# One order of work and one size of transfer: the attention stage of a fused attention, soft-MoE and SwiGLU kernel

## The chip, the core and the metric

The kernel runs on one core of a Trainium2 chip. The metric is the device time of one execution in microseconds (us). One execution of each kernel is also recorded by the hardware profiler; the rows shown below come from that record. The engines are PE (matrix products and transposes), DVE, ACT and POOL (element work), and SP, which here only issues transfers.

## What is computed

Three layers follow each other. The inputs q, k, v are float32, 8 batches x 8 heads x 576 positions x 64.

```python
# 1. attention inside chunks of 64 positions
scores = q_c @ k_c.T / sqrt(64)
attn = exp(scores - rowmax); attn /= attn.sum(-1) + 1e-9
out = attn @ v_c
x = out as 4608 tokens x 512
# 2. soft mixture of 8 experts with 4 slots each, hidden 1024
logits = x @ phi                       # 4608 x 32
d = softmax of logits over the tokens; slot_input = d.T @ x
slot_out[e] = relu(slot_input[e] @ w1[e]) @ w2[e]
c = softmax of logits over the slots;  x = c @ slot_out
# 3. SwiGLU with weights of 512 x 1536
out = (silu(x @ w_gate) * (x @ w_val)) @ w_out
```

## The kernel before, in words

The 4608 tokens are 36 tiles of 128 tokens. The attention stage works on pairs of tiles, 18 pairs in all (`NP = NTILE // 2`). Text below numbers the pairs 0 to 17.

The instructions of every engine stand in the order in which the Python code emits them; no scheduler moves them. Each engine takes its own in that order and waits where a value or a buffer is not there yet. All transfers are issued by SP, in order too: a transfer that waits holds up those behind it.

The steps of a pair, with the names of their tiles and their lines:

- `emit_scores` (L321): 64 small products on PE into `s_ps` (L328), then on DVE a maximum `m` (L336) and a subtraction to `ssb` (L338). Behind a tile's products stands the load of the q and k tile that takes its buffer (`load_qk`, L284).
- `emit_pt` (L347), once for each tile: four transposes of `ssb` into `pt_ps` (L351), and the exponential on ACT (L353).
- `emit_pv` (L358): the products with v into `xa_ps` and `xb_ps` (L365), with the load of the next v tile that takes the buffer (`load_v`, L287), and the normalisation on DVE to `x_sb` (L381 to L388).
- `emit_xt` (L395), once for each tile: four transposes of `x_sb` into `xt_ps` (L401), copied by ACT (L403).
- For a group of four tiles: `emit_logits` (products of `xt` with phi into `lt_ps`, L420, a maximum on DVE, exponentials on ACT, the last of them the copy `lt_all`, L453), then `emit_et` (one transpose into `e_ps`, L466) and `emit_si` (products of the exponentials with `x_sb` into `si_ps`, L484, added up by DVE).
- `spread_v` (L316): v must stand in a block-diagonal form; POOL copies the lower 64 rows to their place (L318) and clears where they were (L319).

The PSUM tiles `pt_ps`, `xt_ps`, `lt_ps`, `e_ps` and `si_ps` take turns in a pool of three buffers (`ps_t`).

The loop at L545 emits, in turn `k` (with `a = k - 1`): the v products of pair `a`; logits or slot sums of an earlier group; the score transposes of pair `k`; the scores of pair `k + 1` and the spread of its v; the x transposes of pair `a - 1`; `emit_et`. q, k and v have buffers for four tiles each. The text calls the stretch from one pair's v products to the next a turn. In three of four turns `pump(1)` (L141) also issues the load of an expert weight (1 MB): sixteen buffers of the pool `wp` are filled while attention runs. When the loop is over, the q, k, v buffers become four more weight buffers (`wx`, L572).

After the loop a tail (L576 to L599) finishes the last x transposes, the last two groups and the maximum over all tokens. The expert stage (L758) takes the weights in the order `order`, L130, and each weight buffer that it frees takes a further load. The SwiGLU stage follows (L921 on); the change does not touch it.

Of the kernel before, what the change touches and what calls it, by code (L numbers as in the profile page):

```python
# [8 lines left out]
F32 = mybir.dt.float32  # L9
# [24 lines left out]
def tile_attn_softmoe_swiglu(  # L34
# [10 lines left out]
    out: bass.AP,  # L45
):
    nc = tc.nc
    D = v.shape[4] - 1
    NT, DM = out.shape
    E = w1.shape[0]  # L50
    NS = phi.shape[1]
    NTILE = NT // 128
# [4 lines left out]
    VW = D + 1  # L57
# [210 lines left out]
    with tc.manual_schedule():  # L268
# [8 lines left out]
        pa = ExitStack()  # L277
        ring = pr.enter_context(tc.tile_pool(name="ring", bufs=1, side="right"))

        NK, NV = 4, 4  # L280
        qk_sb = [ring.tile([128, 2, 4, 128], F32, name=f"qk{i}") for i in range(NK)]
        v_bd = [ring.tile([128, 2, 2, 4, VW], F32, name=f"vbd{i}") for i in range(NV)]

        def load_qk(u):  # L284
            nc.sync.dma_start(out=qk_sb[u % NK], in_=qk[u])

        def load_v(u):  # L287
            nc.sync.dma_start(out=v_bd[u % NV][:, 0], in_=v[u])

        for i in (0, 1):  # L290
            load_qk(i)
        for i in (0, 1):
            load_v(i)
        for i in (2, 3):
            load_qk(i)
        nc.sync.dma_start(out=phi_sb, in_=phi.rearrange("(k p) s -> p k s", p=128))
        for i in (2, 3):
            load_v(i)

        make_identity(nc, ident)  # L300
        for i in range(NV):
# [11 lines left out]
        sc_t = {}  # L313
        row = [slice(0, 64), slice(64, 128)]

        def spread_v(u):  # L316
            t = v_bd[u % NV]
            nc.gpsimd.tensor_copy(out=t[row[1], 1], in_=t[row[1], 0])  # L318
            nc.gpsimd.memset(t[row[1], 0], 0.0)  # L319

        def emit_scores(p):  # L321
            sp = ps_s.tile([128, 2, 2, 4, 64], F32, tag="s", name="s_ps")
            for n in range(8):
                i, j = 2 * p + n // 4, n % 4
                for a in range(2):
                    for cc in range(2):
                        t = slice(64 * cc, 64 * cc + 64)
                        nc.tensor.matmul(  # L328
                            out=sp[t, a, n // 4, j, :], lhsT=qk_sb[i % NK][row[a], 0, j, t],
                            rhs=qk_sb[i % NK][row[a], 1, j, t], start=True, stop=True,  # L330
                        )
                if j == 3 and i + NK < NTILE:
                    load_qk(i + NK)
            sv = sp.rearrange("p a t j k -> p a (t j) k")
            m = sm.tile([128, 2, 8], F32, tag="m", name="m", bufs=1)
            nc.vector.tensor_reduce(out=m, in_=sv, axis=AX.X, op=ALU.max)  # L336
            ssb = atp.tile([128, 8, 2, 64], F32, tag="ssb", name="ssb", bufs=1)
            nc.vector.tensor_tensor(  # L338
                out=ssb.rearrange("p n a k -> p a n k"), in0=sv,
                in1=m.unsqueeze(3).to_broadcast([128, 2, 8, 64]), op=ALU.subtract,  # L340
            )
            for t in range(2):
                sc_t[2 * p + t] = ssb[:, 4 * t:4 * t + 4]
# [14 lines left out]
        def emit_pv(p):  # L358
            xa = ps_x.tile([128, 2, 512], F32, tag="xa", name="xa_ps")
            xb = ps_x.tile([128, 512], F32, tag="xb", name="xb_ps")  # L360
            banks = [xa[:, 0], xa[:, 1], xb]
            for n in range(8):
                i, j = 2 * p + n // 4, n % 4
                for cc in range(2):
                    nc.tensor.matmul(  # L365
                        out=banks[n // 3][64 * cc:64 * cc + 64, (n % 3) * 2 * VW:(n % 3 + 1) * 2 * VW],
                        lhsT=pt_t[i][:, j, 64 * cc:64 * cc + 64],
                        rhs=v_bd[i % NV][:, :, cc, j, :],
                        start=True, stop=True,
                    )  # L370
                if j == 3:
                    pt_t.pop(i)
                    if i + NV < NTILE:
                        load_v(i + NV)
            x = xp.tile([128, 2, 512], F32, tag="x", name="x_sb")
            rec = sm.tile([128, 16, 1], F32, tag="rec", name="rec", bufs=2)
            av = xa[:, :, 0:6 * VW].rearrange("p b (h d) -> p b h d", d=VW)
            bv = xb[:, 0:4 * VW].rearrange("p (h d) -> p h d", d=VW)
            ra, rb = rec[:, 0:12].rearrange("p (b h) o -> p b h o", b=2), rec[:, 12:16]
            xv = x.rearrange("p t (h d) -> p (t h) d", d=D)  # L380
            nc.vector.tensor_scalar(out=ra, in0=av[:, :, :, D:VW], scalar1=1e-9, scalar2=None, op0=ALU.add)  # L381
            nc.vector.tensor_scalar(out=rb, in0=bv[:, :, D:VW], scalar1=1e-9, scalar2=None, op0=ALU.add)
# [28 lines left out]
        lt_t = {}  # L411
        lx_t = {}

        def emit_lmm(g, lt=None):
            if lt is None:
                lt = ps_t.tile([128, 512], F32, tag="t", name="lt_ps")
            lt_t[g] = lt
            for kk in range(4):
                for jt in range(4):
                    nc.tensor.matmul(  # L420
# [35 lines left out]
        def emit_logits(g):  # L456
            emit_lmm(g)
            emit_lmax(g)
            emit_lexp(g)
# [77 lines left out]

        warm(6)
        spread_v(0)
        spread_v(1)  # L540
        emit_scores(0)
        load_gv0(0, wp)
        warm(4)
        NP = NTILE // 2
        for k in range(NP + 1):  # L545
            a = k - 1
            if a >= 0:
# [1 line left out]
            if k == NP:  # L549
                break  # L550
            if a >= 3 and a % 2:
                emit_logits((a - 3) // 2)
            elif a >= 4:
                emit_si((a - 4) // 2)
            emit_pt(2 * k)
            emit_pt(2 * k + 1)
            if k + 1 < NP:
                emit_scores(k + 1)
                spread_v(2 * k + 2)
                spread_v(2 * k + 3)  # L560
            if a >= 1:
                emit_xt(2 * a - 2)
                emit_xt(2 * a - 1)
            if a >= 3 and a % 2:
                emit_et((a - 3) // 2)
            if k == 0 or k % 4 != 3:
                pump(1)
            elif k + 1 == NP - 2:
# [450 lines left out]
```

## Time and profile before

| What | Value |
|---|---|
| Time, median of 3 runs | 545.08 us (544.49 to 547.83) |
| The profiled execution's own time | 543.5 us |
| Its span, first to last instruction | 541.7 us |
| PE busy | 521.3 us, 96% of the span |
| DVE busy | 406.7 us, 75% |
| ACT, POOL busy | 260.4 us and 252.9 us |
| Granted PE clock, mean | 0.996 |
| Read from HBM | 80.95 MB |
| Transfers of q and k | 36 of 512 KB, landing 6.6 us after the issue (median) |
| Transfers of v | 36 of 260 KB, landing after 7.5 us |
| Transfers of the expert weights | w1: 16 of 1 MB, 9.3 us; w2: 15 of 1 MB, 13.5 us |

How to read it: a share of busy time is a mean over stages with different limits. Up to about 119 us the kernel is in the attention loop, to 130 us in the tail, to 170 us in the expert stage, and from there in SwiGLU. A wait is put down to whatever came last. PE can be shown as busy in a stage whose length something else sets, since a product that waits for its weights inside a group of products is merged into it.

### The profile page before, as it was taken

To read this page: it belongs to the slowest core of one execution; us is meant where nothing else is said; L and a number is where in the kernel's file an instruction comes from. 1 tells how busy PE (TensorE), PEld (TensorE's weight loads), DVE (VectorE), ACT (ScalarE), POOL (GpSimd) and SP (SyncE) were. 2 spreads that over 40 slices of the span, in tenths; PEclk is the share of its full clock that TensorE was granted. 3 is DMA by queue.
4 is the path that set the end of the run, shared out by engine and by line. 5 is a ranking of instruction groups with operands and counts; after the bars stand their busy time and mean duration, and the time that the engine had idled before them with its cause. 6 is when DMAs were issued, how large, how long until landed. Compare 5 with 4: busy or idle time off the path is not lost.

```text
span 541.7 us, 11039 instructions
## 1 busy us (share of the span) xinstructions
PE 521.3 (96%) x4389; PEld 409.8 (76%) x4389; DVE 406.7 (75%) x673; ACT 260.4 (48%) x504; POOL 252.9 (47%) x252
## 2 busy tenths in 40 slices
PE   7899999998998889999999999999999999999997
PEld 6778887873335568888888888888888888888885
DVE  5778987864766999888898889989898943433554
ACT  1344533342447766666565555545654533333331
POOL 3333343321002576576566756656664743343342
PEclk9999999999999989999999999999999999999999
DMA  8999999999999502020202220222000000222344
GB/s 324 404 358 398 348 405 347 413 416 400 421 416 417 247 1 77 2 78 2 77 1 77 77 79 0 79 79 77 0 1 0 3 0 1 77 79 77 113 179 174
DMA packets 23762, 91.09 MB, mean 168 GB/s; under 512 B 3104, under 2 KB 3104, under 8 KB 17696
## 3 DMA queue, kind: packets, MB, share of 16 engines
q1 hardware_dynamic: 23712, 90.40, 43.1%
q8 instruction: 34, 0.56, 0.4%
q14 instruction: 16, 0.13, 0.1%
HBM read 80.95 MB, written 9.44 MB: 167 GB/s over the span
## 4 chain that ended last, share of the span: by engine, by line
PE 81%; DVE 9%; DMA 6%; issue 2%; ACT 1%; POOL 0%; SPq 0%; ACTq 0%; DVEq 0%
PE o L891 18%; PE o L893 18%; PE o L892 18%; DMA w2t<-in_moe_w_dram 6%; PE v_ps L847 4%; PE g_ps L847 4%; PE xa_ps L365 4%; PE xt_ps L401 3%; PE s_ps L328 3%; PE pt_ps L351 2%; PE gg_ps L828 2%; PE si_ps L484 1%; DVE ssb L338 1%; DVE m L336 1%; PE h_ps L652 1%
## 5 line engine op out<-in xcount | busy, mean ns | idle before, releaser
L860 POOL TENSOR_TENSOR lo_sb<-s_sb,hi_sb 128x512 fp32r<-128x512 f32 x106 | 140.5, 1326 | 130.9 <-ACT hi_sb L859 127.9
L891 PE MATMUL o<-whl,hi_sb 128*128 128x512 f32 x428 | 167.7, 392 | 2.5 <-DVE part L900 2.5
L893 PE MATMUL o<-whl,lo_sb 128*128 128x512 f32 x428 | 167.2, 391 | 0.5 <-POOL lo_sb L860 0.5
L892 PE MATMUL o<-whl,hi_sb 128*128 128x512 f32 x428 | 167.1, 390 | 0.0
L850 ACT ACTIVATE s_sb<-g_ps 128x512 f32<-128x512 f32 (+1 forms) x110 | 64.7, 590 | 149.9 <-PE g_ps L847 147.7
L851 DVE TENSOR_TENSOR s_sb<-s_sb,v_ps 128x512 f32<-128x512 f32 (+1 forms) x110 | 74.0, 674 | 74.5 <-ACT s_sb L850 73.2
L891 PEld LDWEIGHTS o<-whl,hi_sb 128*128 128x128 f32 x428 | 80.6, 188 | 22.2 <-DVE part L900 4.5
L893 PEld LDWEIGHTS o<-whl,lo_sb 128*128 128x128 f32 x428 | 80.6, 188 | 17.8 <-POOL lo_sb L860 0.9
L892 PEld LDWEIGHTS o<-whl,hi_sb 128*128 128x128 f32 x428 | 80.6, 188 | 16.3
L859 ACT ACTIVATE hi_sb<-s_sb 128x512 fp32r<-128x512 f32 (+1 forms) x110 | 67.6, 616 | 0.8 <-DVE s_sb L851 0.8
L904 DVE TENSOR_TENSOR part<-part,o 128x512 f32<-128x512 f32 x92 | 57.1, 677 | 2.6 <-PE o L893 2.6
L318 POOL COPY vbd<-vbd 64x520 f32<-64x520 f32 x36 | 22.3, 619 | 69.9 <-DMA vbd<-in_v_dram 56.2
L213 POOL TENSOR_TENSOR mt<-mt,ex 128x512 f32<-128x512 f32 x32 | 39.5, 1234 | 27.5 <-PE g_ps L847 13.8
L200 DVE SCALAR_TENSOR_TENSOR ex<-raw,ex 128x512 uint16<-128x512 uint16 x32 | 47.2, 1477 | 0.1
L847 PE MATMUL v_ps<-c_t,g_st 128*128 128x512 f32 (+1 forms) x110 | 42.5, 390 | 0.8 <-DMA raw<-in_moe_w_val_dram 0.5
L847 PE MATMUL g_ps<-c_t,g_st 128*128 128x512 f32 (+1 forms) x110 | 42.4, 389 | 0.1
L353 ACT ACTIVATE pt<-pt_ps 128x512 f32<-128x512 f32 x36 | 19.5, 596 | 36.2 <-PE pt_ps L351 36.2
L195 DVE SCALAR_TENSOR_TENSOR mt<-mt,raw 128x512 f32<-128x512 f32 x32 | 34.9, 1090 | 0.0
L336 DVE TENSOR_REDUCE m<-s_ps 128x16 f32<-128x1024 f32 x18 | 22.0, 1224 | 14.8 <-PE s_ps L328 14.7
L187 DVE TENSOR_SCALAR mt<-raw 128x512 int32<-128x512 int32 x32 | 32.9, 1027 | 0.0
L365 PE MATMUL xa_ps<-vbd,pt 128*64 128x130 f32 x432 | 28.2, 277 | 0.0
L403 ACT ACTIVATE xt<-xt_ps 128x512 f32<-128x512 f32 (+1 forms) x36 | 19.3, 596 | 13.7 <-PE xt_ps L401 10.2
(138 smaller groups left out, 664.2 us busy)
## 6 DMA issues: line engine op xcount, KB each, us to landing
qk<-in_qk_dram SPq DMA_DIRECT2D x36, 512.0 KB, 6.6
w1t<-in_moe_w_dram SPq DMA_DIRECT2D x16, 1024.0 KB, 9.3
w2t<-in_moe_w_dram SPq DMA_DIRECT2D x15, 1024.0 KB, 13.5
vbd<-in_v_dram SPq DMA_DIRECT2D x36, 260.0 KB, 7.5
out_dram<-part SPq DMA_DIRECT2D x36, 256.0 KB, 2.2
raw<-in_moe_w_out_dram SPq DMA_DIRECT2D x6, 1024.0 KB, 7.1
raw<-in_moe_w_gate_dram SPq DMA_DIRECT2D x5, 1024.0 KB, 4.8
raw<-in_moe_w_val_dram SPq DMA_DIRECT2D x5, 1024.0 KB, 5.1
```

What stands on the lines that cost most here:

```text
L200: nc.vector.scalar_tensor_tensor(out=ex, in0=hh, scalar=0x8000, in1=ex, op0=ALU.bitwise_and, op1=ALU.bitwise_or)
L213: nc.gpsimd.tensor_tensor(out=m, in0=m, in1=p, op=ALU.mult)
L365: nc.tensor.matmul(out=banks[n // 3][64 * cc:64 * cc + 64, (n % 3) * 2 * VW:(n % 3 + 1) * 2 * VW], lhsT=pt_t[i][:, j, 64 * cc:64 * cc + 64 ...
L847: nc.tensor.matmul(out=ps[:, k], lhsT=g_st[:, c, gi, ff:ff + 128], rhs=c_blk(b)[:, k], start=True, stop=True)
L850: nc.scalar.activation(out=s[:, k], in_=gp[:, k], func=ACTF.Silu)
L851: nc.vector.tensor_tensor(out=s[:, k], in0=s[:, k], in1=vp[:, k], op=ALU.mult)
L859: nc.scalar.activation(out=hi[:, k], in_=s[:, k], func=ACTF.Copy)
L860: eng.tensor_tensor(out=lo[:, k], in0=s[:, k], in1=hi[:, k].bitcast(F32), op=ALU.subtract)
L891: nc.tensor.matmul(out=a, lhsT=hi[:, ts], rhs=w_hi, start=first, stop=False)
L892: nc.tensor.matmul(out=a, lhsT=hi[:, ts], rhs=w_lo, start=False, stop=False)
L893: nc.tensor.matmul(out=a, lhsT=lo[:, ts], rhs=w_hi, start=False, stop=last)
L904: nc.vector.tensor_tensor(out=p[:, t], in0=p[:, t], in1=a, op=ALU.add)
```

## The change

Two things are done in the attention stage.

First, transfers. The arrays of q and k, and of v, are laid out by pairs on the host side, and one transfer brings a pair: 1 MB for q and k, 520 KB for v. There are two buffers of a pair each in place of four of a tile, so the memory is the same. Only the very first pair of q and k still comes in two transfers. A pair's load is issued when the whole pair in its buffer has been used. The spread of v is one copy and one clearing for a pair.

Second, the order in a turn. The x transposes move from the turn's end to the place right behind the v products, with `emit_et` ahead of them. The logits and the slot sums move behind the score transposes, and each is done one turn sooner. So the next-to-last group's logits are done inside the loop, and the tail loses one round of logits with its own PSUM buffer (`lt2`).

```diff
-        NK, NV = 4, 4
-        qk_sb = [ring.tile([128, 2, 4, 128], F32, name=f"qk{i}") for i in range(NK)]
-        v_bd = [ring.tile([128, 2, 2, 4, VW], F32, name=f"vbd{i}") for i in range(NV)]
-        def load_qk(u):
-            nc.sync.dma_start(out=qk_sb[u % NK], in_=qk[u])
-        def load_v(u):
-            nc.sync.dma_start(out=v_bd[u % NV][:, 0], in_=v[u])
+        NK, NV = 2, 2
+        qk_sb = [ring.tile([128, 2, 2, 4, 128], F32, name=f"qk{i}") for i in range(NK)]
+        v_bd = [ring.tile([128, 2, 2, 2, 4, VW], F32, name=f"vbd{i}") for i in range(NV)]
+        def load_qk(p):
+            for t in (slice(0, 1), slice(1, 2)) if p == 0 else (slice(0, 2),):
+                nc.sync.dma_start(out=qk_sb[p % NK][:, t], in_=qk[p][:, t])
+        def load_v(p):
+            nc.sync.dma_start(out=v_bd[p % NV][:, 0], in_=v[p])
...
         def emit_scores(p):
...
-                if j == 3 and i + NK < NTILE:
-                    load_qk(i + NK)
+            if p + NK < NP:
+                load_qk(p + NK)
...
         def emit_pv(p):
...
                 if j == 3:
                     pt_t.pop(i)
-                    if i + NV < NTILE:
-                        load_v(i + NV)
+            if p + NV < NP:
+                load_v(p + NV)
...
             if a >= 3 and a % 2:
-                emit_logits((a - 3) // 2)
-            elif a >= 4:
-                emit_si((a - 4) // 2)
-            emit_pt(2 * k)
-            emit_pt(2 * k + 1)
-            if k + 1 < NP:
-                emit_scores(k + 1)
-                spread_v(2 * k + 2)
-                spread_v(2 * k + 3)
+                emit_et((a - 3) // 2)
             if a >= 1:
                 emit_xt(2 * a - 2)
                 emit_xt(2 * a - 1)
-            if a >= 3 and a % 2:
-                emit_et((a - 3) // 2)
+            emit_pt(2 * k)
+            emit_pt(2 * k + 1)
+            if a >= 2 and a % 2 == 0:
+                emit_logits((a - 2) // 2)
+            elif a >= 3:
+                emit_si((a - 3) // 2)
+            if k + 1 < NP:
+                emit_scores(k + 1)
+                spread_v(k + 1)
...
         g = NG - 1
-        lt2 = ps_s.tile([128, 2, 512], F32, tag="s", name="lt_ps")
+        emit_et(g - 1)
         emit_xt(NTILE - 4)
         emit_xt(NTILE - 3)
-        emit_lmm(g - 1, lt2[:, 0])
+        emit_si(g - 1)
         emit_xt(NTILE - 2)
-        emit_lmax(g - 1)
         emit_xt(NTILE - 1)
-        emit_lexp(g - 1)
-        emit_lmm(g, lt2[:, 1])
-        emit_et(g - 1, False)
+        emit_lmm(g)
         emit_lmax(g)
         emit_lexp(g)
-        emit_zst(g - 1)
         emit_m1()
-        emit_si(g - 1)
         emit_et(g, False)
```

The order on PE in the middle of the loop, before: two turns, from the v products of an odd pair (`xa_ps`) on. `vbd` and `qk` are the buffers of v and of q and k, one for a tile.

```order
L420 MATMUL lt_ps<-xt,phi_sb 32x128 x16
L351 MATMUL pt_ps<-ident,ssb 128x128 x8
L328 MATMUL s_ps<-qk_99 64x64 x16
L328 MATMUL s_ps<-qk_100 64x64 x16
L401 MATMUL xt_ps<-ident,x_sb 128x128 x8
L466 MATMUL e_ps<-ident,et 128x128
L365 MATMUL xa_ps<-vbd_101,pt 64x130 x8
L365 MATMUL xa_ps<-vbd_102,pt 64x130 x4
L365 MATMUL xb_ps<-vbd_102,pt 64x130 x4
L484 MATMUL si_ps<-x_sb,e 32x512 x4
```

And the same place now:

```order
L363 MATMUL xa_ps<-vbd_99,pt 64x130 x12
L363 MATMUL xb_ps<-vbd_99,pt 64x130 x4
L399 MATMUL xt_ps<-ident,x_sb 128x128 x8
L349 MATMUL pt_ps<-ident,ssb 128x128 x8
L416 MATMUL lt_ps<-xt,phi_sb 32x128 x16
L326 MATMUL s_ps<-qk_97 64x64 x32
L363 MATMUL xa_ps<-vbd_100,pt 64x130 x12
L363 MATMUL xb_ps<-vbd_100,pt 64x130 x4
L462 MATMUL e_ps<-ident,et 128x128
L399 MATMUL xt_ps<-ident,x_sb 128x128 x8
L349 MATMUL pt_ps<-ident,ssb 128x128 x8
L480 MATMUL si_ps<-x_sb,e 32x512 x4
```

The scores, which had the x transposes behind them, are now the last work of a turn, and the logits stand between the score transposes and the scores.

On POOL, the spread of one pair of v before, and then now; the number behind `vbd` is the buffer:

```order
L318 COPY vbd2_103<-vbd2_103 64x520
L319 MEMSET vbd2_103 64x520
L318 COPY vbd3_104<-vbd3_104 64x520
L319 MEMSET vbd3_104 64x520
```

```order
L316 COPY vbd1_100<-vbd1_100 64x1040
L317 MEMSET vbd1_100 64x1040
```

Two short steps for each tile became one of twice the length for the pair, behind one transfer.

## Rows read from the trace of the kernel before

**Rows 1.** Chain of waits, 128 to 180 us; start, length, what.

```profile
153.21 15.51 DMA w2t<-in_moe_w_dram
168.76 0.69 PE so_ps L695 x13
```

**Rows 2.** Stretches: engines' busy us, granted clock, transfer share, GB/s (last).

```profile
12.00:18.00 6.00, 5.23 (x126) 4.59 (x120) 5.17 (x9) 1.09 (x2) 1.57 (x3) 1.00 1.03 408
84.00:86.00 2.00, 2.00 (x73) 1.93 (x73) 0.80 (x2) 1.94 (x7) 1.88 (x4) 1.00 0.67 227
88.00:90.00 2.00, 2.00 (x21) 1.01 (x16) 1.17 (x3) 0.10 (x1) 1.88 (x4) 1.00 1.03 338
96.00:102.00 6.00, 5.90 (x119) 4.33 (x118) 4.08 (x11) 2.92 (x9) 1.71 (x4) 1.00 1.02 410
132.00:138.00 6.00, 6.00 (x56) 1.85 (x52) 3.98 (x19) 1.14 (x3) 0.33 (x3) 1.00 0.99 386
162.00:168.00 6.00, 6.00 (x56) 1.78 (x48) 3.53 (x6) 4.48 (x7) 1.48 (x1) 1.00 1.02 416
```

**Rows 3.** Timeline of SP's issues, 80 to 86 us; start, time to issue, what.

```profile
80.77 1.27 SPq L288 DMA_DIRECT2D vbd<-in_v_dram  x2
84.76 1.10 SPq L285 DMA_DIRECT2D qk<-in_qk_dram  x2
85.92 0.42 SPq L89 DMA_DIRECT2D w1t<-in_moe_w_dram  x1
```

**Rows 4.** Timeline of PE, two turns: start, us, what, idle before.

```profile
66.94 1.55 PE L365 MATMUL xa_ps<-vbd,pt 128*64 128x130 f32 x24
...
68.86 1.08 PE L420 MATMUL lt_ps<-xt,phi_sb 128*32 128x128 f32 x32
69.87 1.09 PE L351 MATMUL pt_ps<-ident,ssb 128*128 128x128 f32 x8
70.89 1.16 PE L328 MATMUL s_ps<-qk 64*64 64x64 f32 x64
72.29 1.14 PE L401 MATMUL xt_ps<-ident,x_sb 128*128 128x128 f32 x8 [0.24 <-ACT lt_all L453]
73.27 0.32 PE L466 MATMUL e_ps<-ident,et 128*128 128x128 f32 x1
73.52 1.55 PE L365 MATMUL xa_ps<-vbd,pt 128*64 128x130 f32 x24
...
79.58 1.55 PE L365 MATMUL xa_ps<-vbd,pt 128*64 128x130 f32 x24
```

**Rows 5.** Timeline of PE, an earlier odd turn, first row to next turn.

```profile
28.89 1.55 PE L365 MATMUL xa_ps<-vbd,pt 128*64 128x130 f32 x24
...
35.50 1.55 PE L365 MATMUL xa_ps<-vbd,pt 128*64 128x130 f32 x24
```

**Rows 6.** Timeline of DVE, beside the first turn of rows 4.

```profile
72.12 1.23 DVE L336 TENSOR_REDUCE m<-s_ps 128x16 f32<-128x1024 f32 x1 [0.59 <-PE s_ps L328]
73.38 1.23 DVE L338 TENSOR_TENSOR ssb<-s_ps,m 128x1024 f32<-128x1024 f32 x1
```

**Rows 7.** Timeline of PE, up to the v products of pair 2.

```profile
18.74 1.09 PE L351 MATMUL pt_ps<-ident,ssb 128*128 128x128 f32 x8 [0.68 <-DVE ssb L338]
...
21.37 0.50 PE L328 MATMUL s_ps<-qk 64*64 64x64 f32 x18 [0.69 <-issue]
...
22.83 1.55 PE L365 MATMUL xa_ps<-vbd,pt 128*64 128x130 f32 x24
```

**Rows 8.** Timeline of POOL: the spread of pair 2, first and last.

```profile
21.30 0.61 POOL L318 COPY vbd<-vbd 64x520 f32<-64x520 f32 x1 [7.67 <-DMA vbd<-in_v_dram]
...
23.12 0.53 POOL L319 MEMSET vbd<- 64x520 f32 x1
```

**Rows 9.** The tile vbd, 20 to 120 us: its transfers, one for a tile.

```profile
DMA to landing us min/median/max: 5.1/7.5/9.2
```

**Rows 10.** Timeline of PE in the tail: the last group's logits.

```profile
123.62 1.08 PE L420 MATMUL lt_ps<-xt,phi_sb 128*32 128x128 f32 x32 [1.02 <-ACT lt_all L453]
```

More of the change, by code (lines that the diff above doesn't have):

```diff
@@ L47, in tile_attn_softmoe_swiglu @@
     nc = tc.nc
-    D = v.shape[4] - 1
+    D = v.shape[5] - 1
     NT, DM = out.shape
@@ L278, in tile_attn_softmoe_swiglu @@
         ring = pr.enter_context(tc.tile_pool(name="ring", bufs=1, side="right"))
-        NK, NV = 4, 4
-        qk_sb = [ring.tile([128, 2, 4, 128], F32, name=f"qk{i}") for i in range(NK)]
-        v_bd = [ring.tile([128, 2, 2, 4, VW], F32, name=f"vbd{i}") for i in range(NV)]
-        def load_qk(u):
-            nc.sync.dma_start(out=qk_sb[u % NK], in_=qk[u])
-        def load_v(u):
-            nc.sync.dma_start(out=v_bd[u % NV][:, 0], in_=v[u])
[L290 to L295, printed above, removed]
+        NK, NV = 2, 2
+        NP = NTILE // 2
+        qk_sb = [ring.tile([128, 2, 2, 4, 128], F32, name=f"qk{i}") for i in range(NK)]
[5 more added lines that the diff above has]
+            nc.sync.dma_start(out=v_bd[p % NV][:, 0], in_=v[p])
+        load_qk(0)
+        load_v(0)
+        load_qk(1)
         nc.sync.dma_start(out=phi_sb, in_=phi.rearrange("(k p) s -> p k s", p=128))
-        for i in (2, 3):
-            load_v(i)
+        load_v(1)
         make_identity(nc, ident)
@@ L314, in tile_attn_softmoe_swiglu, with spread_v @@
         row = [slice(0, 64), slice(64, 128)]
-        def spread_v(u):
-            t = v_bd[u % NV]
+        def spread_v(p):
+            t = v_bd[p % NV]
             nc.gpsimd.tensor_copy(out=t[row[1], 1], in_=t[row[1], 0])
@@ L323, in emit_scores @@
             for n in range(8):
-                i, j = 2 * p + n // 4, n % 4
+                j = n % 4
                 for a in range(2):
@@ L328, in emit_scores @@
                         nc.tensor.matmul(
-                            out=sp[t, a, n // 4, j, :], lhsT=qk_sb[i % NK][row[a], 0, j, t],
-                            rhs=qk_sb[i % NK][row[a], 1, j, t], start=True, stop=True,
-                        )
-                if j == 3 and i + NK < NTILE:
-                    load_qk(i + NK)
+                            out=sp[t, a, n // 4, j, :], lhsT=qk_sb[p % NK][row[a], n // 4, 0, j, t],
+                            rhs=qk_sb[p % NK][row[a], n // 4, 1, j, t], start=True, stop=True,
+                        )
+            if p + NK < NP:
+                load_qk(p + NK)
             sv = sp.rearrange("p a t j k -> p a (t j) k")
@@ L367, in emit_pv @@
                         lhsT=pt_t[i][:, j, 64 * cc:64 * cc + 64],
-                        rhs=v_bd[i % NV][:, :, cc, j, :],
+                        rhs=v_bd[p % NV][:, :, n // 4, cc, j, :],
                         start=True, stop=True,
@@ L412, in tile_attn_softmoe_swiglu, with emit_lmm @@
         lx_t = {}
[L414 to L417, printed above, removed]
+        def emit_lmm(g):
+            lt = lt_t[g] = ps_t.tile([128, 512], F32, tag="t", name="lt_ps")
             for kk in range(4):
@@ L539, in tile_attn_softmoe_swiglu @@
         spread_v(0)
-        spread_v(1)
         emit_scores(0)
@@ L543, in tile_attn_softmoe_swiglu @@
         warm(4)
-        NP = NTILE // 2
         for k in range(NP + 1):
@@ L993 @@
             a = _np.stack([qt.reshape(NU, 128, 4, 128), kt.reshape(NU, 128, 4, 128)], 2)
+            a = a.reshape(NU // 2, 2, 128, 2, 4, 128).transpose(0, 2, 1, 3, 4, 5)
         elif name == "v":
@@ L996 @@
             a = _np.concatenate([a, _np.ones(a.shape[:-1] + (1,), a.dtype)], -1).transpose(0, 2, 1, 3, 4)
+            a = a.reshape(NU // 2, 2, 128, 2, 4, D + 1).transpose(0, 2, 1, 3, 4, 5)
         elif name in ("moe_w1", "moe_w2"):
```

## The prediction

> **What bounds the kernel now.** I read the chain of waits first, from the expert stage backwards. The SwiGLU stage can start only when the last expert weight is there: two links of over 15 us on transfers of w2 stand before 168.76 us [rows 1]. What follows is bound by PE, and the change does not touch it. So the change is worth what it does to the moment when that last weight lands.
>
> Then the stretches, to see when the transfers are the limit [rows 2]. From 96 us on they run at 410 GB/s or more with a share of 1.02, and only 132 to 138 us shows 386. A queue that is full all the time cannot end sooner unless it was filled sooner or moves faster. Ahead of 96 us it was not always full: in one of four turns no weight is loaded, and behind such a turn there is a hole. The last hole is at 84 to 86 us, 227 GB/s and a share of 0.67. It ends when SP asks for the next q and k at 84.76 us and a weight at 85.92 us [rows 3]. So the end of the expert stage hangs on the time of these two issues, and they hang on how far PE has come in the loop.
>
> Then the timeline of PE. A turn has v products (1.92 us, from 66.94 to 68.86), logits or slot sums (1.01), score transposes (1.02), scores (about 1.1) and x transposes (0.98), in sum 6.0, and in every second turn 0.25 for `e_ps` [rows 4]. An even turn takes 6.06 us: PE has no slack there. An odd turn takes 6.58, so 0.27 of it is waiting; the first such turn takes 6.61 [rows 5], 0.30 of it waiting. The row of the x transposes names the cause: 0.24 us for the copy `lt_all`, which has to give back a PSUM buffer.
>
> The profiled execution took 543.5 us, 1.6 below the median of 545.08. Sums are made against it, and 1.6 is added at the end.
>
> **The change, step by step**, up to the last hole.
>
> *The wait of the odd turns.* Between `lt_ps` and the third use of that buffer now stand scores and v products, some 3 us, in place of score transposes and scores, and ACT is through with its copy by then. I take the wait as gone: four odd turns before the hole, 4 x 0.29 = -1.15 us.
>
> *What the moved x transposes do to the score transposes.* These need `ssb`, which is there 3.72 us after the scores began (70.89 [rows 4] to 74.61 [rows 6]). In the new order scores, v products and x transposes take 1.1 + 1.92 + 0.98 = 4.0 us ahead of them. The cover was one logits longer; 0.3 us is left. Nothing, then, unless DVE comes late to the scores.
>
> *The logits, one turn sooner.* One more round stands before any place in the loop: +1.01 us [rows 4]. The tail gives it back, but the tail is behind the hole.
>
> *v by pairs, first time.* Pair 2 is the first whose v is reloaded. Its first tile had landed by 21.30 us, both were spread at 23.12 + 0.53 = 23.65, and the v products of the first tile began at 22.83, before the second was ready [rows 7, 8]. Now nothing can begin before both are spread. The queue is full there (408 GB/s [rows 2]), so the second tile's 0.27 MB land 0.65 us behind the first, at 21.95; the spread of both takes 2.35 (23.65 - 21.30); start at 24.3, 1.5 us later than before. PE would be there earlier, since the x transposes fill the 0.68 us in which it waited for `ssb` [rows 7]. At the other end, if the larger transfer lands sooner, the cost is 0. I take +1.1, nearer to the row.
>
> *v by pairs, later.* A pair's load is issued when its buffer's v products are done, and is needed two turns later: 2 x 6.18 - 1.92 = 10.4 us, and less 2.35 for the spread 8.1 are left to land. A tile took 7.5 us in the median and 9.2 at most [rows 9]. The load of a pair is issued 0.95 later than that of its first tile and lands 0.65 behind it, so 7.2 in the median and 8.9 at most: in most turns nothing, in the worst 0.8. I take +0.3 before the hole, between 0 and 1.0. [...]
>
> *The issues move in the turn.* Scores, and the load of q, k and the weight behind them, now come after the x transposes: about 1.0 us later in the turn. v does not move.
>
> At the hole v is thus asked for 1.1 + 1.0 - 1.15 + 0.3 = 1.3 us later, q, k and the weight 2.3 later. The hole is as long as q, k and the weight make it, less what the later v puts into it; I take the middle, **+1.8 us**, between -0.1 and +3.4.
>
> *Behind the hole.* After it the rate is low even at a full share: 338 GB/s at 88 to 90 us with 1.03 [rows 2]. Two us at 416 in its place would be 0.4 us; if all of 86 to 94 us were like this row and larger transfers cured it, 1.5. I take -0.4. The low stretch at 132 to 138 us costs (416 - 386) / 416 x 6 = 0.4 us [rows 2]; it comes when the tail keeps PE from freeing weight buffers. The tail loses one logits (1.01 us) and a wait of 1.02 [rows 10] and so comes no later than before: -0.4. Six MB of q, k and v are still to come behind the hole; at 416 in place of 410 GB/s that is -0.2. The SP issues saved (36 of about 0.4 us) cost nothing now, since SP waits, and POOL's work stays the same in sum.
>
> Sum: 1.8 - 0.4 - 0.4 - 0.2 = +0.8 us, so 544.3 for an execution like the profiled one, **545.9 us** for the median. The tail's saving does not reach the end otherwise: the weights are not there yet.
>
> **The rivals.**
>
> *Larger transfers make the queue faster (542.9 us).* For it: 408 to 410 GB/s with q, k and v in the mix against 416 with weights alone, and the 338 above [rows 2]. Then pair 2 costs nothing, v is never late, the issues come 0.9 us later, and behind the hole 1.5 + 0.4 + 0.2 come back: -1.2; and if the first hole's delay in the turn is hidden by work still in the queue, -2.2, which with 1.6 is 542.9. Against it: 408 is only 2% short. [...]
>
> *v is late in nearly every turn (551.2 us, slower).* Place: the start of the v products, behind POOL. If the landing is over 8.1 us behind the end of the v products, PE waits for the whole excess every second turn. At 9.2 us, the longest of a tile, plus 0.2 for the issue, two turns must last 1.92 + 0.2 + 9.2 + 2.35 = 13.7, so one 6.8 against some 6.3 now: 0.48 for each of the ten turns with a weight in the queue, 4.8, and 1.3 for pair 2 make 6.1: 549.6, and 551.2 as a median. For it: 9.2 occurs. Against it: the median is 7.5, and every fourth turn drains the queue.
>
> *Nothing moves (545.1 us).* The queue takes up every shift of the issues, as it is several us deep, and the gains behind the hole cancel what is left.
>
> **How the numbers follow.** The forecast gets 0.55, the faster queue 0.22, the late v 0.12, no movement 0.11. The forecast's own range is from 543 to 548.5, by the ends of its terms (-2.2 to +3.4). The range from 542.5 to 549.5 leaves out the lower tail of the faster queue (0.05), most of the late v (0.09) and a little of the forecast (0.05). A change of 1%, 5.4 us, is what a measurement here can tell from none, as the runs before spread over 3.3 us. Faster by that means under 539.6, which no term reaches: 0.03. Slower means over 550.5: the upper two thirds of the late v, 0.08. The rest, 0.89, is no change.
>
> **What would show it.** The turns should last 6.05 and 6.3 us in place of 6.06 and 6.6, without a wait for `lt_all`. The v products of pair 2 should wait for POOL and begin at 23.5 to 24.3 us, those of pair 11 1 to 1.5 us later than 79.58 [rows 4]. The hole behind the turn without a weight should be longer than before, the last w2 should land at 169 to 170 us in place of 168.7, and the first expert product should begin no later than before. I am wrong if the last w2 lands over 2 us sooner, or if PE waits for `vbd` in most turns.

## The result, and the profile after

| | Before | After |
|---|---|---|
| Median of the first comparison | 546.59 us (9 runs) | 550.13 us (546.31 to 552.53, 9 runs) |
| Ratio, 95% interval | | 1.0081 [1.0057, 1.0106] |
| A second comparison (e11, below) | 545.71 us (9 runs) | 547.70 us (8 runs), 1.0029 [1.0000, 1.0058] |
| Profiled execution, span | 543.5, 541.7 us | 550.13, 548.3 us |
| First expert product | 130.76 us | 137.84 us |
| End of the expert stage (`sos`) | 169.54 us | 176.16 us |
| Packets of the data queue | 23,712 | 18,672 |

The ratios are those on record, not quotients of the medians. The change costs between nothing and 1%, about 0.5% over both comparisons. 545.9 had been forecast, with a range from 542.5 to 549.5: the first median lies above that range, the second inside it. In the first comparison the time goes with the granted clock: the nine executions after have a mean clock from 0.988 (552.08 and 552.53 us) to 1.000 (546.31 us), 0.991 in the median. The eight of the second have 0.997, the nine of before beside them 0.993. The profiled execution after is 6.6 us longer than that of before, more than the medians differ. The 6.6 us are all there when the expert stage ends, and SwiGLU is as long as it was.

Two turns of PE after, from the v products of pair 8 on, answer to [rows 4]; the columns are start, length, what, and in brackets the wait ahead of it with what ended it:

```profile
63.98 1.55 PE L363 MATMUL xa_ps<-vbd,pt 128*64 128x130 f32 x24 [0.19 <-POOL vbd L317]
...
65.90 1.09 PE L399 MATMUL xt_ps<-ident,x_sb 128*128 128x128 f32 x8
66.83 1.07 PE L349 MATMUL pt_ps<-ident,ssb 128*128 128x128 f32 x8
67.84 1.08 PE L416 MATMUL lt_ps<-xt,phi_sb 128*32 128x128 f32 x32
68.85 1.16 PE L326 MATMUL s_ps<-qk 64*64 64x64 f32 x64
69.94 1.55 PE L363 MATMUL xa_ps<-vbd,pt 128*64 128x130 f32 x24
```

An undisturbed turn lasts 5.96 us (69.94 - 63.98), the next kind 6.06 at best, with no wait for `lt_all`. The moved order works. But many turns are disturbed, in two ways. The same view at other places:

```profile
22.85 0.58 PE L326 MATMUL s_ps<-qk 64*64 64x64 f32 x25 [0.75 <-issue]
24.37 2.55 PE L363 MATMUL xa_ps<-vbd,pt 128*64 128x130 f32 x24 [0.94 <-POOL vbd L317]
...
86.57 0.92 PE L399 MATMUL xt_ps<-ident,x_sb 128*128 128x128 f32 x7 [1.72 <-issue]
...
90.42 1.55 PE L363 MATMUL xa_ps<-vbd,pt 128*64 128x130 f32 x24
...
99.35 0.33 PE L363 MATMUL xa_ps<-vbd,pt 128*64 128x130 f32 x1 [1.43 <-issue]
...
113.71 1.78 PE L363 MATMUL xa_ps<-vbd,pt 128*64 128x130 f32 x14 [2.69 <-issue]
```

The row at 90.42 is the v products of pair 12, with which the turn ends that held the last hole before. The kernel before had them here:

```profile
86.23 1.55 PE L365 MATMUL xa_ps<-vbd,pt 128*64 128x130 f32 x24
```

Four v products wait for POOL: 0.94 at 24.37, 1.19 at 51.27, 0.38 at 57.67 and 0.19 at 63.98, in sum 2.7 us; none waited before. And five groups stand still in their middle with "issue" as the releaser, that is, for nothing that the profile of PE shows: 0.45 at 16.70, and the four above, 7.0 us in sum. Before there were three (0.69 [rows 7], 0.68, 0.25), 1.6 us. The text calls these standstills. Both kinds have a sequel in the stretches (columns as in [rows 2]):

```profile
24.00:30.00 6.00, 5.63 (x56) 5.07 (x60) 3.82 (x7) 1.40 (x3) 2.33 (x3) 0.72 0.94 359
...
90.00:96.00 6.00, 6.00 (x164) 5.34 (x157) 4.86 (x11) 2.07 (x4) 2.02 (x2) 1.00 0.72 275
96.00:102.00 6.00, 4.57 (x81) 4.03 (x72) 4.44 (x9) 2.12 (x8) 1.36 (x2) 1.00 1.01 415
102.00:108.00 6.00, 6.00 (x123) 4.67 (x121) 4.39 (x9) 2.12 (x6) 1.70 (x2) 1.00 0.91 341
...
114.00:120.00 6.00, 6.00 (x66) 4.61 (x65) 2.15 (x7) 2.34 (x5) 2.01 (x2) 0.76 0.94 363
...
138.00:144.00 6.00, 6.00 (x52) 1.72 (x48) 3.09 (x16) 1.42 (x4) 0.22 (x2) 1.00 0.90 351
...
162.00:168.00 6.00, 6.00 (x53) 2.74 (x57) 4.56 (x21) 2.65 (x7) 0.25 (x2) 1.00 1.01 411
```

Two of these stretches, 102 to 108 and 114 to 120 us, are holes that the kernel before did not have:

```profile
102.00:108.00 6.00, 6.00 (x145) 5.22 (x144) 5.42 (x9) 2.17 (x4) 1.87 (x4) 1.00 1.03 413
...
114.00:120.00 6.00, 5.69 (x68) 4.43 (x64) 3.08 (x7) 2.18 (x4) 2.19 (x4) 1.00 1.02 421
```

Behind the two waits at 22 to 24 us and behind the standstill of 2.69 us the granted clock is 0.72 and 0.76 in the stretches above; from 25 to 28 us and from 114 to 116 us alone it is 0.50. The 24 v products of pair 2 take 2.55 us where they took 1.55 [rows 7]. In both places the rest of the turn is 1.6 us longer than the same work elsewhere (7.57 against 5.96; 7.09 from 113.71 to 120.80, against 6.06 less some 0.55 for the products already done), 3.2 us together.

SP's issues round the last hole answer to [rows 3], and the spread of pair 2 on POOL to [rows 8]:

```profile
82.60 0.33 SPq L287 DMA_DIRECT2D qk<-in_qk_dram  x1
84.56 0.33 SPq L290 DMA_DIRECT2D vbd<-in_v_dram  x1
90.55 0.33 SPq L287 DMA_DIRECT2D qk<-in_qk_dram  x1
90.93 0.42 SPq L89 DMA_DIRECT2D w1t<-in_moe_w_dram  x1
```

```profile
22.25 1.05 POOL L316 COPY vbd<-vbd 64x1040 f32<-64x1040 f32 x1 [8.10 <-DMA vbd<-in_v_dram]
23.36 0.96 POOL L317 MEMSET vbd<- 64x1040 f32 x1
```

The time that a pair of v took to land (the tile `vbd`, 20 to 120 us) answers to [rows 9]:

```profile
DMA to landing us min/median/max: 4.1/7.9/9.4
```

The chain of waits after, in the expert stage, answers to [rows 1]:

```profile
137.84 1.92 PE h_ps L640 x16
...
170.31 5.76 PE so_ps L683 x57
...
176.16 0.48 ACT sos L769
```

The two links on transfers of w2 are gone. From 137.84 us on the chain is PE alone, 38.32 us long. Before it took 38.78 us from 130.76 to 169.54, with the waits for w2 in it. So PE's own work was only 0.5 us shorter than the way over the weights. The weights are level with it after: in the trace the last w2 lands at 175.34 us (168.72 before), and the first product with it begins at 175.38. PE and the weights come to the end together, both 6.6 us later.

**Where the 7.1 us up to the first expert product went**: a later start of the first scores, +0.75 (5.19 against 4.44 us); standstills, 7.0 - 1.6 = +5.4; v late behind POOL, +2.7; work at the lower clock, +3.2; the order itself, -3.4 (e5 against e10, with a standstill of 0.34 us of e5 in it); the tail, -1.7 (12.17 us from the v products of pair 17, at 125.67, to the first expert product, against 13.84). Sum +6.95. The term of the order is taken over from other runs, so the sum is a check and not a measurement.

### The profile page after: what moved, and what is told of

It is laid out like the page before. It is cut to its first block, busy times and chain, and to the rows that moved or that the text cites. A ratio compares the mean times of both kernels' runs of the same rounds, so it can differ in the third digit from the quotient of the medians.

```text
span 548.3 us, 10908 instructions
## 1 busy us (share of the span) xinstructions
PE 521.7 (95%) x4389; PEld 412.5 (75%) x4389; DVE 405.9 (74%) x671; ACT 261.2 (48%) x504; POOL 248.8 (45%) x216
## 3 DMA queue, kind: packets, MB, share of 16 engines
q1 hardware_dynamic: 18672, 90.40, 42.3%
## 4 chain that ended last, share of the span: by engine, by line
PE 86%; DMA 5%; DVE 4%; issue 2%; POOL 2%; SPq 0%; ACT 0%; DVEq 0%; POOLq 0%; ACTq 0%
PE o L879 18%; PE o L880 17%; PE o L881 17%; DMA vbd<-in_v_dram 5%; PE xa_ps L363 5%; PE v_ps L835 4%; PE g_ps L835 4%; PE so_ps L683 3%; PE h_ps L640 3%; PE xt_ps L399 3%; PE pt_ps L349 2%; PE s_ps L326 2%; PE gg_ps L816 2%; PE lt_ps L416 2%; PE xb_ps L363 1%
## 5 line engine op out<-in xcount | busy, mean ns | idle before, releaser
L879 PEld LDWEIGHTS o<-whl,hi_sb 128*128 128x128 f32 x428 | 80.7, 188 | 22.3 <-DVE part L888 4.5
L316 POOL COPY vbd<-vbd 64x1040 f32<-64x1040 f32 x18 | 18.9, 1050 | 81.9 <-DMA vbd<-in_v_dram 56.8
L363 PE MATMUL xa_ps<-vbd,pt 128*64 128x130 f32 x432 | 30.6, 289 | 6.8 <-issue 4.1
L363 PEld LDWEIGHTS xa_ps<-vbd,pt 128*64 128x64 f32 x432 | 25.4, 141 | 8.8 <-issue 4.7
```

What stands on the lines that cost most here:

```text
L363: nc.tensor.matmul(out=banks[n // 3][64 * cc:64 * cc + 64, (n % 3) * 2 * VW:(n % 3 + 1) * 2 * VW], lhsT=pt_t[i][:, j, 64 * cc:64 * cc + 64 ...
L879: nc.tensor.matmul(out=a, lhsT=hi[:, ts], rhs=w_hi, start=first, stop=False)
```

## The experiments

Theories at the outset: the loss lies in the transfers by pairs, in the moved order, or in both; within the transfers, in their number, their rows, or the time of their issue. Later ones: the standstills come of the full queue or of the order, and finally (theory I) they are waits of PE for its own instructions.

**e1, the order alone.** The new order and tail, transfers and spreads by tile as before; shown against the kernel after.

```diff
-        NK, NV = 2, 2
+        NK, NV = 4, 4
...
-        def load_v(p):
-            nc.sync.dma_start(out=v_bd[p % NV][:, 0], in_=v[p])
+        def load_v(u):
+            nc.sync.dma_start(out=v_bd[u % NV][:, 0], in_=v[u])
...
-                spread_v(k + 1)
+                spread_v(2 * k + 2)
+                spread_v(2 * k + 3)
```

> The new order of a turn and of the tail, with q, k and v still brought tile by tile and spread tile by tile. Theory A (the large transfers are what costs: PE stands still for 1.4 to 2.7 us at three places in the changed kernel, in the middle of a group of products and with no wait that the profile names, and waits 2.7 us in sum for the spread of v): this run is not slower than the kernel before, ratio 0.992 to 1.000, turns without a wait last 6.0 us as in the changed kernel, and no standstill on PE is over 0.8 us. Theory B (the new order is what costs, because the load of q and k and of the weight is issued later in the turn and PE reaches the same places at another time): ratio 1.005 to 1.010, and the standstills are there.

546.5 us, ratio 1.0028 [0.9999, 1.0056]. v is never late. PE's timeline has this:

```profile
82.28 0.44 PE L365 MATMUL xb_ps<-vbd,pt 128*64 128x130 f32 x4 [2.25 <-issue]
```

One standstill of 1.31 us at 22.20, this one, and 0.26 at 105.44. The first expert product begins at 128.80, 2 us sooner than before, and `sos` at 169.42, no sooner: now the last weight is late (the stage takes 40.6 us instead of 38.3). The order alone brings PE through the loop sooner and gains nothing, as the weights come no sooner. Neither theory is met: standstills are there, as theory B has it, but the ratio lies below its range.

**e2, the transfers alone.** Old order and tail, q, k and v by pairs; shown against the kernel after (the tail left out).

```diff
-                emit_et((a - 3) // 2)
-            if a >= 1:
-                emit_xt(2 * a - 2)
-                emit_xt(2 * a - 1)
+                emit_logits((a - 3) // 2)
+            elif a >= 4:
+                emit_si((a - 4) // 2)
             emit_pt(2 * k)
             emit_pt(2 * k + 1)
-            if a >= 2 and a % 2 == 0:
-                emit_logits((a - 2) // 2)
-            elif a >= 3:
-                emit_si((a - 3) // 2)
             if k + 1 < NP:
                 emit_scores(k + 1)
                 spread_v(k + 1)
+            if a >= 1:
+                emit_xt(2 * a - 2)
+                emit_xt(2 * a - 1)
+            if a >= 3 and a % 2:
+                emit_et((a - 3) // 2)
```

> The transfers by pairs, one buffer and one spread for a pair, in the old order of a turn and the old tail. Theory A (large transfers cost): ratio 1.005 to 1.015, with standstills of PE over 1 us in the middle of groups, and waits for the spread of v at pairs 2 and some of 6 to 12. Theory B (order costs): ratio 0.998 to 1.003, standstills no longer than 0.7 us.

546.45 us, 1.0024 [1.0000, 1.0049]. Its profiled execution took 553.3 us, far over its median, so its trace is used only for the standstills (one, of 2.18 us) and for the length of the expert stage. The two parts, 0.28% and 0.24%, add up to 0.5%, but neither interval lies clear of no change, so how the loss divides between them is not shown.

**e3, each pair in two transfers**, issued together at the pair's end.

```diff
-            for t in (slice(0, 1), slice(1, 2)) if p == 0 else (slice(0, 2),):
+            for t in (slice(0, 1), slice(1, 2)):
...
-            nc.sync.dma_start(out=v_bd[p % NV][:, 0], in_=v[p])
+            for t in (slice(0, 1), slice(1, 2)):
+                nc.sync.dma_start(out=v_bd[p % NV][:, 0, t], in_=v[p][:, t])
```

> The changed kernel, but each pair's q and k, and each pair's v, come in two transfers, one for a tile, issued one behind the other when the pair's buffer is free; buffers, spread and order as changed. Theory A1 (the size of one transfer costs, as something else of PE's has to wait behind it): the standstills over 1 us are gone, the waits for the spread stay, ratio 1.000 to 1.004. Theory A2 (the later issue for a whole pair costs, not the size of a transfer): same as the changed kernel, 1.006 to 1.010, with the standstills.

551.19 us, 1.013 [1.0098, 1.0161]: the slowest of the four. PE's waits from 20 to 120 us (us in total, times, longest):

```profile
PE xa_ps L364 <- POOL vbd L318: 6.6, 6, 2.1
PE s_ps L327 <- issue: 0.9, 1, 0.9
```

Here v is late in six turns, by up to 2.1 us, which is the mechanism of the slower rival, and only one standstill is left. SP took up to 2.13 us for the two issues of v, where two of q and k in the kernel before took 0.80 (at 78.22 us). Neither range of the theories is met. Against e4 (1.0060), which issues one transfer at the same moment, two are slower. Whether the late moment itself costs, or the two issues, this run does not part.

**e4, one transfer for a pair, but in rows of a tile** (4 KB for q and k, 2 KB for v; the arrays in DRAM stay by tiles).

```diff
-                nc.sync.dma_start(out=qk_sb[p % NK][:, t], in_=qk[p][:, t])
+                nc.sync.dma_start(
+                    out=qk_sb[p % NK][:, t].rearrange("p t c j d -> p t (c j d)"),
+                    in_=qk[p][t].rearrange("t p c j d -> p t (c j d)"))
```

> The changed kernel with one transfer for a pair, but q, k and v lie by tiles in memory, so that the transfer has rows of 4 KB and 2 KB, twice as many, in place of 8 KB and 4 KB. Theory A1 in the form that the length of a row costs: standstills over 1 us gone, ratio 1.000 to 1.004. In the form that the size of the whole transfer costs: as the changed kernel, 1.006 to 1.010.

547.9 us, 1.0060 [1.0034, 1.0086]. Standstills of 1.31, 0.78, 1.46 and 2.14 us at the same places as after, v late by 2.5 us in sum. The length of the rows is not the cause.

**e5, after, without expert weights in the loop** (they are loaded behind it, so the whole is much longer).

```diff
-            if k == 0 or k % 4 != 3:
+            if k < 2:
                 pump(1)
-            elif k + 1 == NP - 2:
-                pump(2)
```

> The changed kernel without the loads of expert weights inside the loop; all of them come after it, so the time of the whole is worse by some 25 to 35 us and says nothing; the loop is what is looked at. Theory F (a full transfer queue makes PE stand still, at fixed counts of its instructions, and makes v late): no standstill over 0.5 us, no wait of the v products for the spread but at pair 2, and turns of 5.96 and 6.05 us throughout from pair 3 to pair 17. Theory O (the order or the larger spread is itself the cause): the standstills at about the 1614th, 1867th and 2119th product and waits for the spread remain.

569.57 us. In the loop the transfers run at some 265 GB/s (268 at 48 to 54 us); turns last 5.96 and 6.05 us but for one of 6.81, v is late at pair 2 alone (1.25), and two standstills are left, 0.71 and 0.34. The 0.71, over the 0.5 of theory F, is at 24.02 us, where the weights of the first two turns are still under way. So the order does not make the standstills by itself (theory O falls): with the queue lightly loaded they are short (0.34 to 0.71 us), with a full one long, up to 2.69 us after (theory F).

**e6, after, with v by tile** (four buffers, two spreads; q and k by pairs).

```diff
-        NK, NV = 2, 2
+        NK, NV = 2, 4
...
-                spread_v(k + 1)
+                spread_v(2 * k + 2)
+                spread_v(2 * k + 3)
```

> The changed kernel with v alone back to transfers, buffers and spreads by tile; q and k stay by pairs, the order stays. Theory V (the late v is what the change costs beyond noise): no wait for the spread over 0.4 us after pair 2, ratio 1.000 to 1.004. Theory S (the standstills are the larger part and come with a transfer of 1 MB for q and k): standstills of 1 us and more remain, ratio 1.004 to 1.008.

547.73 us, 1.0063 [1.0042, 1.0083]. v is late by 1.3 us in sum. PE's timeline:

```profile
83.41 0.59 PE L365 MATMUL xb_ps<-vbd,pt 128*64 128x130 f32 x3 [2.41 <-issue]
...
84.20 1.92 PE L401 MATMUL xt_ps<-ident,x_sb 128*128 128x128 f32 x8
```

One long standstill, and behind it the x transposes at about half the pace (1.92 us instead of 1.04). That is nearer to theory S than to V. It is no clean test of V: half of the wait for v is left (0.41 and 0.92 us).

**e7 and e8, the weights evenly spread.** If the turns without a weight make the damage, with their hole and the rush behind it, half weights in all turns should help: one or two of 512 KB in each, in the new order (e7, made from e1) and in the old (e8, from the kernel before).

```diff
+        if by_half[0]:
+            step = 1024
...
-            if k == 0 or k % 4 != 3:
+            if k < 2:
                 pump(1)
-            elif k + 1 == NP - 2:
-                pump(2)
+            else:
+                by_half[0] = True
+                n = (4 if k == 15 else 2) if k >= 15 else 2 if k % 2 == 0 or k == 3 else 1
+                while len(half_q) < n:
+                    pump(1)
+                flush(n)
+                by_half[0] = False
```

> The new order with transfers by tile (as e1_order), and the expert weights of the loop in half transfers, one or two in every turn, in place of one whole in three of four turns. Theory F (bursts over what the queue can carry make PE stand still and v late, and holes in the queue set the end): standstills under 0.5 us, no hole below 350 GB/s between 30 and 96 us, last w2 2 to 4 us sooner, ratio 0.993 to 0.998. Theory N (the queue's filling in the loop does not matter): as e1_order, 1.000 to 1.005.

> The kernel before with the expert weights of the loop in half transfers, one or two in every turn. Theory F: the holes behind the turns without a weight are gone, the last w2 lands 1 to 4 us sooner, ratio 0.993 to 0.999. Theory N: 0.999 to 1.002.

e7: 549.07 us, 1.0082 [1.0065, 1.0100]; e8: 546.65, 1.0033 [1.0017, 1.0049]. Both are slower than before, so the expected gain did not come: the last w2 of e8 landed at 172.17 us, over 3 us later than before, and e7 has standstills of 0.57, 2.25 and 2.15 us. PE's waits in e8, 20 to 120 us:

```profile
PE s_ps L341 <- issue: 2.3, 4, 0.9
PE lt_ps L433 <- issue: 2.1, 2, 1.5
PE xa_ps L378 <- issue: 0.9, 1, 0.9
```

In the old order, with by-tile transfers, standstills grow from 1.6 to over 5 us when weights are under way in every turn. It may be that the turns without a weight are where late transfers catch up; no run shows that by itself.

**What a standstill is.** The profile's third part has a queue of its own for instructions, 34 packets of 0.56 MB in sum in both kernels, counted like the data against 16 engines (0.4% of their span). Short stretches of the trace give the start of each packet. The queue's row for 84.0 to 84.3 us of after (packets, MB, share):

```profile
q8 instruction: 1, 0.02, 21.1%
```

That packet starts at 84.14; the standstill of 1.72 us ends at 86.57, 2.43 later. In the kernel before, for 80.5 to 80.7 us, and the standstill that follows in PE's timeline:

```profile
q8 instruction: 1, 0.02, 34.2%
```

```profile
83.09 0.98 PE L351 MATMUL pt_ps<-ident,ssb 128*128 128x128 f32 x7 [0.25 <-issue]
```

The packet starts at 80.58, 2.51 us ahead. Over all thirteen profiles there are 45 standstills of 0.2 us or more between 14 and 126 us; each ends 2.2 to 2.6 us behind the start of a packet of this queue, though packets come only about every 6 us. And counted in the trace's records of PE products from the start of the program (the `x24` of a row are 24 records) they stand on one grid: 221, 347, 473, ... 1610, 1863, 2115, all whole multiples of 126 to 127 records apart. In e1, e6 and e7 the late ones come 5 to 7 records sooner. With the weight load of each product (4389 records of each kind in the whole profile) these are some 253 instructions. The last three runs test this.

**e9, the grid shifted**: 20 tiny products of two records each ahead of the loop.

```diff
         warm(6)
+        tiny = ps_t.tile([128, 512], F32, tag="t", name="tiny")
+        for _ in range(20):
+            nc.tensor.matmul(out=tiny[:, 0:16], lhsT=ident, rhs=ident[:, 0:16], start=True, stop=True)
```

> The changed kernel with 20 tiny products (128x16, each two records on PE) more ahead of the loop, where PE waits for the first q and k anyway. All later work on PE stands 40 records further on in its program. Theory I (the standstills with no releaser are waits for PE's own instructions, which come in blocks of some 253 instructions, about 126 products, over the same transfer engines as the data): the standstills stay at the same counts from the program's start (346 to 347, 1606 to 1618, 1861 to 1871, 2119 to 2123, where there are any) and so stand 40 records earlier in the work of a turn, in other groups than xt_ps, xa_ps and xa_ps; each ends 2.3 to 2.6 us after the start of a packet of the instruction queue, as all of them did so far. Rival P (what stands there in the turn causes them): same groups and places as in the changed kernel, so counts of 387, 1654, 1907 and 2159. Time 548 to 552 us by both.

560.04 us (2 runs), 1.0274 [1.0165, 1.0383]: the time was expected wrongly, since the 40 records took 8.55 us, not the idle 1.5, and the loop began 7 us later. What the run is for holds. In PE's timeline:

```profile
52.63 0.27 PE L363 MATMUL xb_ps<-vbd,pt 128*64 128x130 f32 x1 [2.16 <-issue]
...
93.75 0.33 PE L326 MATMUL s_ps<-qk 64*64 64x64 f32 x5 [2.38 <-issue]
```

Standstills at counts 599, 852, 1231, 1357 and 1611, on the same grid, so 40 records earlier in the work: 1611 now falls into the scores, where after 1610 fell into the x transposes. The place in the turn does not make them (rival P falls). Of the four counts expected only this one had a standstill; the others are at further points of the grid. (The counts in the expectations of e5, e9 and e11 are a few higher than the trace has them.)

**e10, before, without weights in the loop** (the edit of e5).

> The kernel before without the expert weights in the loop (they are loaded behind it), as the control for the same edit of the changed kernel. Theory I: PE has no standstill over 0.8 us here either, turns last 6.06 and 6.58 us with the wait for lt_all, and from pair 3 to pair 17 the v products take some 4 us longer than the 84.6 us of the changed kernel without weights: the moved order is worth that when the queue leaves it alone. Rival (the order is worth nothing by itself): within 1 us of each other. Time 566 to 573 us, since the weights come late.

568.92 us. The v products of pairs 3 and 17 in e10, and then in e5:

```profile
28.55 1.55 PE L365 MATMUL xa_ps<-vbd,pt 128*64 128x130 f32 x24
...
115.72 1.54 PE L365 MATMUL xa_ps<-vbd,pt 128*64 128x130 f32 x23
```

```profile
31.82 1.55 PE L363 MATMUL xa_ps<-vbd,pt 128*64 128x130 f32 x24
...
115.54 1.55 PE L363 MATMUL xa_ps<-vbd,pt 128*64 128x130 f32 x24
```

87.17 us against 83.72: the moved order is worth 3.4 us over 14 turns where the queue leaves it alone. But e5 reached pair 3 later by 3.3 us, 2.5 of it before its first v products (13.80 against 11.28), the rest with the v of pair 2, which it waited for.

**e11, after once more.**

> The changed kernel, once more. Theory I: the standstills are at the same counts of products (347, near 1612, near 1865, near 2120), though not all of them need be there and their lengths may differ by a microsecond, since they hang on how full the queue is at that moment; each ends 2.3 to 2.6 us behind an instruction packet. Rival (accidents of that one execution): other counts. Time 547 to 552 us.

547.7 us, 1.0029 [1.0000, 1.0058]. PE's timeline, two of the standstills:

```profile
84.90 0.93 PE L399 MATMUL xt_ps<-ident,x_sb 128*128 128x128 f32 x7 [1.34 <-issue]
...
111.21 0.99 PE L363 MATMUL xa_ps<-vbd,pt 128*64 128x130 f32 x14 [2.14 <-issue]
```

Seven standstills, 6.2 us in sum, at 221, 347, 1357, 1610, 1863, 2115 and 2241: the places repeat, the lengths vary by half a microsecond. The clock did not fall this time (1.00 from 108 to 120 us; 14 v products in 0.99 us, not 1.78), the first expert product came at 134.98, and the last weight was the bound again (38.88 us to `sos`).

## Why the prediction was wrong

**The step that failed: the sum up to the hole, +1.8 us, and with it that nothing in the loop behind the hole would count.** The sum takes a turn of PE as its work plus the waits for other engines. It has no term for PE's own instructions, though a row shows such a wait, 0.69 us with "issue" [rows 7]; none for a lower clock; and its term for a late v is too small. At the v products of pair 12 it makes 1.1 + 1.0 - 1.15 + 0.3 = 1.3 us. Measured are 4.2 (90.42 against 86.23): v late +2.7, where 1.4 stood; the lower clock behind pair 2 +1.6; standstills +1.3 (2.9 against 1.6); the first scores +0.75; and, as what is left, -2.2 by the order, where -0.1 stood. Pair 11 began 2.9 us later (82.48), not 1 to 1.5. In the trace the weight asked for behind the hole landed 5.3 us later (99.15 against 93.83).

Behind the hole the prediction has the queue full whatever PE does. Two more standstills (1.43 and 2.69 us) and the lower clock behind the second come ahead of the holes at 102 to 108 and 114 to 120 us, and the last w2 came 6.6 us later, at 175.34, where 169 to 170 was forecast. Over the whole loop standstills are +5.4 us in this execution (4.6 in e11), the lower clock 3.2 (none in e11).

e9 and the 45 packets show what a standstill is, e5 and e10 what the order saves without a full queue. That a shorter turn reaches the next place of the grid sooner, while under a full queue the packet starts late, and that the saving so comes back as a standstill, fits these runs; no run shows it by itself. Neither of the prediction's signs of being wrong came: the last w2 did not land sooner, and four v products of eighteen waited for `vbd`.

**What bounds the kernel**: right as read from the chain, but too narrow. The prediction let the first expert product come "no later than before" and so ignored PE's way through the expert stage. That is 38.3 us from the first product in five profiles of different kernels (after, e2, e4, e8, e9), only 0.5 us less than before needed with its waits. Any later end of the loop beyond 0.5 us goes straight to the end.

**The odd turns' wait**: gone, as said, and the even turns gained too. -1.15 us up to the hole was too little: 3.4 us over the loop, a quarter of a microsecond for each turn.

**Score transposes**: still covered, as said; no wait for `ssb` was added in the loop of the profile shown (e11 has one of 0.31).

**Pair 2's v**: it waited behind POOL, as said, and began at 24.37 where 24.3 was forecast, but that close a hit is luck. The load was there later (the spread begins at 22.25, not 21.95), as the loop had begun 0.75 later, and the spread was shorter (2.07 us, 22.25 to 24.32, not 2.35). What followed, the clock at 0.72, had no price.

**v later**: the term was mis-sized. +0.3 us (0 to 1.0) before the hole; measured 1.19 + 0.38 + 0.19 = 1.8 (0.4 in e11). A pair's v landed after 7.9 us in the median and 9.4 at most, against 7.5 and 9.2 for a tile [rows 9]; 7.2 and 8.9 had been estimated.

**The hole**: q and k asked for at 90.55 and the weight at 90.93 us, against 84.76 and 85.92 [rows 3], +5.8 and +5.0 where +2.3 was forecast; 90 to 96 us ran at 275 GB/s. The direction was right. The excess is what PE was late by already, and in it the 1.7 of standstill at 86.57, in the very turn that fills the hole.

**Behind it**: the dip did not go. It now lies at 138 to 144 us, round the later first expert product, with 351 GB/s against 386 [rows 2]. The tail's own saving came (1.7 us of the 2.0). With q, k and v in the mix and a full share the queue ran at 415 GB/s (96 to 102 us) against 410 [rows 2], which is the forecast's -0.2 us and no more. The low rate at a full share stayed (345 GB/s with 1.02 at 84 to 86 us). The weights alone, behind the loop, run at 411 GB/s against 416 [rows 2]. e2 brings q and k in transfers of 1 MB (v in half of that), at a ratio of 1.0024 [1.0000, 1.0049]. Before, 512 KB took 6.6 us to land in the median, while the queue moved 410 GB/s [rows 2], which is 2.7 MB in that time: by this estimate several transfers were under way at once, and the larger ones bought nothing that could be measured.

**The rivals and the range.** The faster queue did not appear. The late v, at 551.2, came near the first median by its number, not by its mechanism: v explains 2.7 us, and e6, which takes half of that away, is not clearly faster. e3 shows that mechanism nearly by itself, at 551.19. The range ended at 549.5 because only v stood behind its upper end.

**What stays open**: why a packet of instructions starts late. The trace shows how late: after PE passes one place of the grid, the packet for the next starts 3.4 to 5.5 us later ahead of the five standstills after, with 393 to 422 GB/s in the two microseconds before it. Where these ran at 264 to 352 GB/s (the packets at 24.11, 31.60, 38.23 and 63.44 us), it started 0.4 to 1.3 us later; one at 89.89 us took 3.2 with 296 GB/s. e9's standstill of 2.16 us fits: its packet started 3.9 us behind the grid place, and 48 to 54 us ran at 421 GB/s. That it waits behind the data is an inference. It is open too what makes the clock fall, in one execution and not in the next. And no kernel tried beats the one before.

## What to carry to other kernels

When a kernel streams its program and its data at once, look for waits of PE in the middle of a group with no releaser, count the instructions between them, and set them beside the packets of the instruction queue; a shorter loop under a full queue may meet them sooner. In the kernel after, five such waits made 7.0 us. Before a stage is called bound by transfers, work out what its engine alone would take from the same start: here the two ways lay 0.5 us apart, and a change that helps one alone is worth at most that much. Loads that are issued later in larger pieces can lose slack even where their number falls: here v came in 18 loads in place of 36 and was late by 2.7 us in sum.

## What the runs showed of the hardware

PE's instructions arrive in packets of some 16.5 KB (0.56 MB in 34), one for 126 to 127 records of PE products of this kernel, and PE goes on 2.2 to 2.6 us behind the start of a packet that it waits for (45 cases of 45). With the weight loads these records are some 253 instructions. The longest wait for one packet was 2.69 us (after).

Waits of PE were followed by a lower granted clock in some places: 0.72 behind waits of 0.75 and 0.94 us and 0.76 behind one of 2.69 (after), 0.78 behind one of 2.16 (e9, 54 to 60 us); behind one of 2.41 (e6) eight x transposes took 1.92 us instead of 1.04. Behind 1.72 and 1.43 us after, 2.14 us in e11 (clock 1.00 in all three) and 2.25 us in e1 (eight x transposes in 1.04 us) the work went on at full pace.

A product of 128x16 ahead of the loop took 0.21 us for each record in e9 (40 in 8.55 us), hardly less than one of 128x128 right ahead of them (12 in 2.93 us, 0.24 each).
